# Softmax sums copied earlier, the first half's high part sooner and weight steps behind other tiles, in a fused attention and feed-forward kernel

## The chip, the cores and the metric

One core of a Trainium2 chip runs the whole program. Its engines run side by side, each through its own list of instructions in order: TensorE (matmuls, PE in the profile, its weight loads PEld), VectorE (DVE), ScalarE (ACT), GpSimd (POOL) and SyncE (SP), which issues most DMAs. The metric is the device time of one execution in microseconds, the median of several; lower is better.

## The reference

Attention over 16 heads of 576 positions and 64 dimensions with rotary embedding, then two feed-forward layers without gates over 1152 tokens (512 to 2048 to 512), the first with ELU, the second with Mish:

```python
q_rot, k_rot = (rotate(q), rotate(k))
scores = scale * np.matmul(q_rot, k_rot.transpose(0, 1, 3, 2))
scores = scores - np.max(scores, axis=-1, keepdims=True)
attn = np.exp(scores)
attn = attn / (np.sum(attn, axis=-1, keepdims=True) + 1e-09)
attn_out = np.matmul(attn, v)
...
x = attn_out.transpose(0, 2, 1, 3).reshape(B * S, H * D)
h = x @ w_in;  g = elu(h);           x = g @ w_out     # first layer
h = x @ w_in2; g = h * tanh(softplus(h)); out = g @ w_out2  # second layer
```

The weights come as 64-bit floats.

## The kernel before

All matmul operands of the feed-forward layers, and q and k, are held as a high part and a low part, and each product is made of three matmuls (high by high, high by low, low by high).

The attention takes the 16 heads in 8 pairs. A pair has 9 tiles of 128 queries (TPP = 9): tiles 0 to 3 are its first half (256 queries of both heads), tiles 4 to 8 its second half (320 queries of both heads; tile 8 holds the last 64 queries of either head). Tile number u counts through all pairs, u = 9 p + i. The engines' orders are written by hand: inside `manual_schedule` each engine executes what the Python loop emits, in that order. One turn of the loop (L573) at u does:

- TensorE: scores of tile u (`do_S`, into `ps_s`, two buffers). In pairs 0 and 1 an even tile issues the scores of two tiles at once, interleaved.
- VectorE: the maximum over the keys of tile u (`do_max`, writes `mn`, L392), and at tiles 4 and 0 the inverse of a finished half's sums (`do_inverse`, writes `rw`).
- TensorE: the transposes of tile u - 3 (LAG = 3): 512 keys into `psT` (L441, two buffers by turns), the last 64 keys into one of four slots of the single `psL` (L442).
- At tile 6, and at tile 2 of the next pair, the spread (`do_spread`, L423): matmuls that lay the inverse sums of a half out over `psA`. They need `psA` free, that is the product R before (L488) done.
- One turn later TensorE begins the weighted sums of that half (`do_av`, L473, two chunks of keys, and three more two turns later), into the same `psA`. Before that ScalarE must have copied the spread sums out of `psA` to R (`do_keep`, L432).
- ScalarE or VectorE copies `psT` to `pt` (`do_evac`, L455 on VectorE for tiles 0, 2, 4 and 8, in the last two pairs 0 and 4; else L457 on ScalarE). Behind tiles 3, 7 and 8 VectorE copies `psL` to `pt` (`do_evac_last`, L467), which frees its slots.
- ScalarE: exp of tile u (`do_exp`, L400), which gives P and its sums.
- After the last chunk of a half VectorE multiplies `psA` by R (`do_x`, L488); ScalarE rounds that to XH (`do_xh`, L492), and GpSimd makes XL, the low part (`do_xl`, L496).

GpSimd also does the rope products for the pair after next (L273 to L277) and the split of q and k of the next pair into high and low (L298, L299), whose results SP's DMAs stack.

In between stand weight steps: a job turns 512 KB of 64-bit weights (`raw`) into high and low parts. It is a product on GpSimd (L95, writes `wu`), three integer operations on VectorE (L99, L103, L107), and at last a rounding copy on ScalarE and a difference on GpSimd (L121, L122). `weight_part` does one such step, and keeps two jobs open, so that the GpSimd product of a job comes as soon as the job before it is opened or done. `PARTS` (L551 to L553) says how many steps stand at the end of which tile. 32 steps, 8 jobs, stand in the attention; the other jobs run in the feed-forward layers.

Of the kernel before, what the change touches and what calls it, by code (L numbers as in the profile page):

```python
# [21 lines left out]
def plain(ap):  # L22
    return ap.bitcast(F32)
# [3 lines left out]
def kernel(  # L27
# [11 lines left out]
    nc = tc.nc  # L39
    NP = qk.shape[0]  # L40
# [12 lines left out]
    TPP = 9  # L53
    NU = NP * TPP
# [76 lines left out]
    def prefetch_weights(n):  # L131
        while loaded[0] < min(len(jobs), opened[0] + n):
            load_weight(jobs[loaded[0]])
            loaded[0] += 1
# [95 lines left out]
    def attention(att, ps, tail):  # L230
# [32 lines left out]
        def load_v(p):  # L263
            v = att.tile([128, 5, 128], F32, tag="v", name="v_t", bufs=2)
            nc.sync.dma_start(out=v, in_=vp[p])
            v_t[p] = v
# [162 lines left out]
        def do_keep(p, g):  # L429
            n = (256, 320)[g]  # L430
            R_t[p, g] = att.tile([128, n], F32, tag=f"R{g}", name=f"R{g}", bufs=1)
            nc.scalar.activation(out=R_t[p, g], in_=psA[:, :n], func=AF.Copy)  # L432
# [11 lines left out]
        def do_evac(u):  # L444
            p, i = divmod(u, TPP)
            tv = psT[u % 2]
            pt = pt_t[0 if i < 4 else 1]
            if tiles[i] is not None:
                h, t = tiles[i]
                o = pt[:, h, 0:4, 128 * (t % 2):128 * (t % 2) + 128]  # L450
            else:
                o = pt[:, :, 0:4, 256:320].rearrange("p h c q -> p c h q")
                tv = tv.rearrange("p c (h q) -> p c h q", h=2)
            if i in (ON_DVE if p < NP - 2 else ON_DVE[::2]):
                nc.vector.tensor_copy(out=o, in_=tv)  # L455
            else:
                nc.scalar.activation(out=o, in_=tv, func=AF.Copy)  # L457

        def do_evac_last(i):
            r = S - 512  # L460
            if i < 8:
                o = pt_t[i // 4][:r, :, 4, 0:256].rearrange("p h (t q) -> p h t q", t=2)
                tv = psL[:r].rearrange("p (t h) q -> p h t q", h=2)
            else:
                o = pt_t[1][:r, :, 4, 256:320]
                tv = psL[:r, 0, :].rearrange("p (h q) -> p h q", h=2)
            nc.vector.tensor_copy(out=o, in_=tv)  # L467
# [12 lines left out]
        def x_parts(p, g):  # L480
            b, hp = divmod(p, HPB)
            q0 = (0, 256)[g]
            q1 = (256, S)[g]
            return R_t[p, g], XH[:, b, hp, q0:q1], XL[:, b, hp, q0:q1]
# [5 lines left out]
        def do_xh(p, g):  # L490
            x, hi, lo = x_parts(p, g)
            nc.scalar.activation(out=hi, in_=x, func=AF.Copy)  # L492

        def do_xl(p, g, eng):
            x, hi, lo = x_parts(p, g)
            eng.tensor_tensor(out=lo, in0=x, in1=plain(hi), op=ALU.subtract)  # L496
# [24 lines left out]
        def keep_warm(n):  # L521
            for _ in range(n):
                nc.tensor.matmul(psA[:, 0:128], lhsT=zero, rhs=zero, start=True, stop=True)
# [13 lines left out]
        def prepare(p, k):  # L537
            if k == 0:
                if p + 1 < NP:
                    load_pair(p + 1)  # L540
                split_alloc(p)
                split_half(p, 2, "kh", "kl")
                stack_k(p)
            elif k == 1:
                split_half(p, 0, "qh", "ql")
                stack_q(p)
            elif p + 1 < NP:
                rope_part(p + 1, 2 if k < 5 else 0, (k - 2) % 3, nc.gpsimd)

        LAG = 3  # L550
        PARTS = {u: 1 for u in (28, 30, 32, 34, 37, 39, 41, 43, 46, 48, 50, 52)}  # L551
        PARTS.update({u: 2 if u % 3 == 2 else 1 for u in range(54, 63)})
        PARTS.update({u: 1 for u in range(63, 71)})  # L553
        plan = {
            6: [("r", 0)], 7: [(0, 0), (0, 1)], 9: [(0, 2), (0, 3), (0, 4)],
            11: [("r", 1)], 12: [(1, 0), (1, 1)], 14: [(1, 2), (1, 3), (1, 4)],
# [9 lines left out]
        ends, spreads = {}, {}  # L566
# [6 lines left out]
        for u in range(max(av_at) + 2):  # L573
            p, i = divmod(u, TPP)
            for k in range(8):
                if p and i == k and p + 1 < NP:
                    prepare(p + 1, k)
            if u == 2:
                load_pair(2)
                split_alloc(1)  # L580
            if i == 8 and p + 1 < NP:
                load_v(p + 1)
            if u == 24:
                prefetch_weights(2)
            if u < NU:
                do_S(u)
            if u < LAG + 4:
                keep_warm(FILL[u])
            for (pp, g) in ends.get(u - 1, []):
                do_x(pp, g)  # L590
            if u < NU:
                do_max(u)
            if u == 1:
                first_lo(*HEAD[3])
            if 0 <= u - LAG < NU:
                do_T(u - LAG)
            if i == 4 and u < NU:
                do_inverse(p, 0)
            if i == 0 and u:
                do_inverse(p - 1, 1)  # L600
            for (pp, g) in spreads.get(u - 1, []):
                if u <= NU:
                    do_keep(pp, g)
            for (pp, g, c) in av_at.get(u, []):
                if g == "r":
                    do_spread(pp, c)
                else:
                    do_av(pp, g, c)
            if u >= NU:
                tail(u - NU, False)  # L610
            if 0 <= u - LAG < NU:
                do_evac(u - LAG)
                if (u - LAG) % TPP in (3, 7, 8):
                    do_evac_last((u - LAG) % TPP)
            for (pp, g) in spreads.get(u, []):
                if u >= NU:
                    do_keep(pp, g)
            if u < NU:
                do_exp(u)
            if u == 1:  # L620
                first_hi(*HEAD[-1])
                first_lo(*HEAD[-1])
                stack_q(0)
                nc.scalar.activation(out=tab[:, 0:2, :], in_=tab[:, 2:4, :], func=AF.Copy, scale=QSCALE)
                rope_half(1, 0, nc.gpsimd)
            if u in (3, 5):
                second_split(2 if u == 3 else 0)
            if u == 5:
                stack_q(1)
            if u in (6, 7, 8):  # L630
                for k in (2 * u - 10, 2 * u - 9):
                    prepare(1, k)
            for (pp, g) in ends.get(u - (1 if u >= NU else 2), []):
                do_xh(pp, g)
                do_xl(pp, g, nc.gpsimd if pp < NP - 1 else nc.vector)
            for _ in range(PARTS.get(u, 0)):
                if njob[0] < 2 * GF:
                    weight_part()
            if u >= NU:
                tmp_pool[0] = att  # L640
                tail(u - NU, True)
                tmp_pool[0] = None
# [225 lines left out]
```

## Time and profile before

| | us |
|---|---|
| median of 3 runs | 578.35 |
| the runs | 578.35, 583.51, 577.58 |
| profiled execution | 578.34 |
| its span, first to last instruction | 576.6 |
| TensorE matmul busy | 554.1 (96%) |
| VectorE, ScalarE, GpSimd busy | 374.1, 276.5, 240.9 |
| granted TensorE clock | 0.999 |

The busy time of an engine is a share of the whole span; a stage's limit has to be looked for in that stage. The attention takes about the first 163 us, the two layers the rest. Starts in the rows are microseconds from the first instruction. The end of a matmul in these rows is modelled, so the distance from one start to the next says more than the printed length.

### The profile page before, as it was taken

What the parts mean: (1) busy time and instruction counts of PE and PEld (TensorE: products, weight loads), DVE (VectorE), ACT (ScalarE), POOL (GpSimd) and SP (SyncE); (2) the same over time, 40 slices, a digit from 0 to 9 for tenths busy, and PEclk for the clock granted to TensorE, in tenths of its full rate; (3) what the DMA queues carried; (4) which work ended last, traced back from release to release, by engine and by line L of the source; (5) the groups of instructions that cost most, each with busy time, mean ns of one, the idle gap of its engine ahead of it and who ended that gap; (6) DMA issues with size and microseconds to landing.
All of it is one profiled execution on the core that took longest, in us unless ns stands there. A gap on an engine that the chain in (4) does not pass through costs nothing.

```text
span 576.6 us, 10135 instructions
## 1 busy us (share of the span) xinstructions
PE 554.1 (96%) x3888; PEld 499.3 (87%) x3888; DVE 374.1 (65%) x607; ACT 276.5 (48%) x512; POOL 240.9 (42%) x227
## 2 busy tenths in 40 slices
PE   7789999998999999999999999999999999999996
PEld 6567767776788999999999999999999998999985
DVE  5666778788845867677777777769934555442221
ACT  3646665666755755654554555534533322322110
POOL 6998889884310232233233232355543332230000
PEclk9999999999999999999999999999999999999999
DMA  6367766646210232222232222243542332100012
GB/s 227 112 190 213 228 202 160 197 121 181 73 38 1 74 110 74 79 106 73 75 111 74 74 81 103 59 138 119 164 124 84 107 99 97 33 14 10 28 64 92
DMA packets 43120, 60.69 MB, mean 105 GB/s; under 512 B 13760, under 2 KB 31936, under 8 KB 42304
## 3 DMA queue, kind: packets, MB, share of 16 engines
q1 hardware_dynamic: 42528, 59.46, 33.5%
q8 instruction: 31, 0.51, 0.4%
q10 hardware_dynamic: 544, 0.59, 0.3%
q14 instruction: 17, 0.14, 0.1%
HBM read 46.20 MB, written 2.36 MB: 84 GB/s over the span
## 4 chain that ended last, share of the span: by engine, by line
PE 86%; DVE 5%; ACT 5%; issue 2%; DMA 1%; POOL 0%; SPq 0%; ACTq 0%; POOLq 0%; DVEq 0%
PE ps_s L183 34%; PE ps_g L682 17%; PE ps_h L711 17%; PE psA L473 7%; PE ps_s L385 7%; PE psT L441 3%; DVE mn L392 2%; ACT P L400 2%; DMA qk_t<-in_qk_dram 1%; ACT R L432 1%; PE psL L442 1%; PE psA L423 1%; DVE pt L467 1%; ACT XH L492 0%; DVE tb L217 0%
## 5 line engine op out<-in xcount | busy, mean ns | idle before, releaser
L392 DVE TENSOR_REDUCE mn<-ps_s 128x1 f32<-128x576 f32 x72 | 54.0, 752 | 30.4 <-PE ps_s L385 30.2
L660 ACT ACTIVATE ta<-ps_s 128x576 f32<-128x576 f32 x32 | 20.8, 649 | 92.7 <-PE ps_s L183 92.7
L400 ACT ACTIVATE P<-ps_s,mn 128x576 f32<-128x576 f32 x72 | 53.2, 738 | 16.0 <-DVE mn L392 15.9
L183 PE MATMUL ps_s<-XH,wi0h 128*128 128x288 f32 x256 | 54.9, 296 | 0.9 <-DVE tb L218 0.9
L183 PE MATMUL ps_s<-XL,wi0h 128*128 128x288 f32 x256 | 54.5, 294 | 0.0
L183 PE MATMUL ps_s<-XL,wi1h 128*128 128x288 f32 x256 | 54.4, 294 | 0.0
L183 PE MATMUL ps_s<-XH,wi0l 128*128 128x288 f32 x256 | 54.4, 294 | 0.0
L183 PE MATMUL ps_s<-XH,wi1l 128*128 128x288 f32 x256 | 54.2, 293 | 0.0
L183 PE MATMUL ps_s<-XH,wi1h 128*128 128x288 f32 x256 | 54.2, 293 | 0.0
L122 POOL TENSOR_TENSOR wi1l<-wu,wi1h 128x512 fp32r<-128x512 f32 x16 | 21.4, 1338 | 78.2 <-ACT wi1h L121 78.2
L99 DVE TENSOR_SCALAR wu<-wu 128x512 int32<-128x512 int32 x64 | 32.8, 513 | 30.4 <-POOL wu L95 30.2
L473 PE MATMUL psA<-pt,v_t 128*64 128x256 f32 (+1 forms) x320 | 45.6, 416 | 6.1 <-ACT R L432 5.8
L107 DVE SCALAR_TENSOR_TENSOR wu<-raw,wu 128x512 int32<-128x512 int32 x64 | 49.0, 765 | 1.7
L122 POOL TENSOR_TENSOR wo0l<-wu,wo0h 128x512 fp32r<-128x512 f32 x16 | 21.8, 1365 | 61.9 <-ACT wo0h L121 50.3
L457 ACT ACTIVATE pt<-psT 128x512 f32<-128x512 f32 x44 | 26.3, 597 | 43.6 <-PE psT L441 43.6
L95 POOL TENSOR_SCALAR wu<-raw 128x512 f32<-128x512 f32 x64 | 45.0, 704 | 5.0
L103 DVE SCALAR_TENSOR_TENSOR wu<-raw,wu 128x512 int32<-128x512 int32 x64 | 45.9, 717 | 1.8
L122 POOL TENSOR_TENSOR wo1l<-wu,wo1h 128x512 fp32r<-128x512 f32 x16 | 22.0, 1375 | 57.3 <-ACT wo1h L121 57.0
L183 PEld LDWEIGHTS ps_s<-XH,wi0h 128*128 128x128 f32 x256 | 41.4, 188 | 3.2 <-DVE tb L218 1.3
L662 DVE TENSOR_TENSOR g<-ta,g 128x576 fp32r<-128x576 f32 x25 | 20.4, 817 | 36.5 <-ACT g L661 36.5
L441 PE MATMUL psT<-idn,P 128*128 128x128 f32 x288 | 43.4, 274 | 0.0
L183 PEld LDWEIGHTS ps_s<-XH,wi1h 128*128 128x128 f32 x256 | 41.7, 188 | 1.2
(146 smaller groups left out, 1408.6 us busy)
## 6 DMA issues: line engine op xcount, KB each, us to landing
raw<-in_w_in_dram SPq DMA_DIRECT2D x32, 512.0 KB, 3.7
raw<-in_w_out_dram SPq DMA_DIRECT2D x32, 512.0 KB, 3.3
qk_t<-in_qk_dram SPq DMA_DIRECT2D x6, 1152.0 KB, 5.4
qa<-qh SPq DMA_DIRECT2D x24, 144.0 KB, 2.7
v_t<-in_vp_dram SPq DMA_DIRECT2D x8, 320.0 KB, 3.1
out_dram<-Y SPq DMA_DIRECT2D x9, 256.0 KB, 2.0
ka<-kh SPq DMA_DIRECT2D x12, 144.0 KB, 2.4
ka<-kl SPq DMA_DIRECT2D x12, 144.0 KB, 2.8
```

The lines of the kernel that those rows point to most:

```text
L95: nc.gpsimd.tensor_scalar(out=u, in0=high.bitcast(F32), scalar1=REBASE, scalar2=0.0, op0=ALU.mult, op1=ALU.add)
L103: nc.vector.scalar_tensor_tensor(out=ui, in0=high, scalar=-0x80000000, in1=ui, op0=ALU.bitwise_and, op1=ALU.bitwise_or)
L107: nc.vector.scalar_tensor_tensor(out=ui, in0=low, scalar=29, in1=ui, op0=ALU.logical_shift_right, op1=ALU.bitwise_or)
L122: nc.gpsimd.tensor_tensor(out=lo, in0=u, in1=plain(hi), op=ALU.subtract)
L183: nc.tensor.matmul(o[:, j, :HS], lhsT=w[:, cc, :], rhs=x[:, b, cc, j * HS:j * HS + HS], start=(k == 0), stop=(k == 3 * NC - 1),)
L385: nc.tensor.matmul(psS[w][:, j, :HS], lhsT=l, rhs=r(slice(j * HS, j * HS + HS)), start=(a == 0), stop=(a == len(passes) - 1),)
L392: nc.vector.tensor_reduce(out=m, in_=psS[u][:, :, :HS], axis=AX.XY, op=ALU.min)
L400: nc.scalar.activation(out=P.rearrange("p (j n) -> p j n", j=2), in_=psS.pop(u)[:, :, :HS], func=AF.Exp, scale=-1.0, bias=mn_t.pop(u), acc ...
L441: nc.tensor.transpose(tv[:, c, :], P[:, c * 128:c * 128 + 128], idn)
L473: nc.tensor.matmul(o[64 * h:64 * h + 64, :n], lhsT=v_t[p][:, c, 64 * h:64 * h + 64], rhs=pt_t[g][:, h, c, :], start=(c == 0), stop=(c == 4),)
L682: nc.tensor.matmul(o[:, j, :HS], lhsT=w[:, e * 128:e * 128 + 128], rhs=gt[:, i, j * HS:j * HS + HS], start=(k == 0), stop=(k == 3 * GF - 1),)
L711: nc.tensor.matmul(o, lhsT=l, rhs=w, start=(k == 0), stop=(k == 3 * GF - 1))
```

## The change

Five edits in the loop over tiles:

1. The copy of the spread sums (`do_keep`) is emitted in the same turn as the spread, ahead of that tile's exp; before, it came one turn later, behind that exp.
2. XH and XL of a first half are emitted one turn after its last chunk, not two. The second half's stay.
3. Behind tile 8 VectorE copies `psL` ahead of `psT`.
4. The weight steps stand in every pair from pair 2 on: one at tiles 3 and 5 and two at tile 7 in pairs 2 to 5; two each at tiles 3, 5, 7 and 8 in pairs 6 and 7. Before, they stood at tiles 1, 3, 5 and 7 of pairs 3 to 5, at all tiles of pair 6 and at tiles 0 to 7 of pair 7. There are 32 steps as before.
5. The first two weight loads are issued at u = 16 (tile 7 of pair 1), not at u = 24.

```diff
-        PARTS = {u: 1 for u in (28, 30, 32, 34, 37, 39, 41, 43, 46, 48, 50, 52)}
-        PARTS.update({u: 2 if u % 3 == 2 else 1 for u in range(54, 63)})
-        PARTS.update({u: 1 for u in range(63, 71)})
+        PARTS = {}
+        for p in range(2, NP):
+            for i, n in ((3, 1), (5, 1), (7, 2)) if p < NP - 2 else ((3, 2), (5, 2), (7, 2), (8, 2)):
+                PARTS[TPP * p + i] = n
...
-            if u == 24:
+            if u == 16:
                 prefetch_weights(2)
...
-            for (pp, g) in spreads.get(u - 1, []):
-                if u <= NU:
-                    do_keep(pp, g)
...
             if 0 <= u - LAG < NU:
+                j = (u - LAG) % TPP
+                if j == 8:
+                    do_evac_last(j)
                 do_evac(u - LAG)
-                if (u - LAG) % TPP in (3, 7, 8):
-                    do_evac_last((u - LAG) % TPP)
+                if j in (3, 7):
+                    do_evac_last(j)
             for (pp, g) in spreads.get(u, []):
-                if u >= NU:
-                    do_keep(pp, g)
+                do_keep(pp, g)
             if u < NU:
                 do_exp(u)
...
-            for (pp, g) in ends.get(u - (1 if u >= NU else 2), []):
-                do_xh(pp, g)
-                do_xl(pp, g, nc.gpsimd if pp < NP - 1 else nc.vector)
+            for (pp, g) in ends.get(u - 1, []) + ends.get(u - 2, []):
+                if (pp, g) in ends.get(u - (2 if g and u < NU else 1), []):
+                    do_xh(pp, g)
+                    do_xl(pp, g, nc.gpsimd if pp < NP - 1 else nc.vector)
```

First place, ScalarE at the start of pair 4 (the numbers behind the names count tiles; R1_ is pair 3's second half, R0_ its first half; P is an exp). Before:

```order
L457 ACTIVATE pt1_86<-psT1_82 128x4x128
L400 ACTIVATE P_1120,sums2_78<-ps_s_1105,mn_1111 128x576
L400 ACTIVATE P_1145,sums2_78<-ps_s_1128,mn_1133 128x576
L492 ACTIVATE XH_61<-R0_1018 128x256
L432 ACTIVATE R1_1162<-psA_84 128x320
L400 ACTIVATE P_1169,sums2_78<-ps_s_1150,mn_1155 128x576
```

After:

```order
L457 ACTIVATE pt1_86<-psT1_82 128x4x128
L400 ACTIVATE P_1131,sums2_78<-ps_s_1116,mn_1122 128x576
L492 ACTIVATE XH_61<-R0_1013 128x256
L432 ACTIVATE R1_1153<-psA_84 128x320
L400 ACTIVATE P_1155,sums2_78<-ps_s_1136,mn_1141 128x576
```

XH and the copy of R stand ahead of the exp of tile 2, no longer behind it.

Second place, VectorE at the same seam (mn is a maximum, psT with 128x4x2x64 is tile 8). Before:

```order
L467 COPY pt1_86<-psL_83 64x2x256
L99 TENSOR_SCALAR wu_894<-wu_894 128x512
L392 TENSOR_REDUCE mn_1133<-ps_s_1128 128x1
L455 COPY pt1_86<-psT1_82 128x4x2x64
L467 COPY pt1_86<-psL_83 64x2x64
L392 TENSOR_REDUCE mn_1155<-ps_s_1150 128x1
L455 COPY pt0_85<-psT0_81 128x4x128
L103 SCALAR_TENSOR_TENSOR wu_894<-raw_756,wu_894 128x512
```

After:

```order
L467 COPY pt1_86<-psL_83 64x2x256
L392 TENSOR_REDUCE mn_1141<-ps_s_1136 128x1
L467 COPY pt1_86<-psL_83 64x2x64
L455 COPY pt1_86<-psT1_82 128x4x2x64
L392 TENSOR_REDUCE mn_1163<-ps_s_1158 128x1
L455 COPY pt0_85<-psT0_81 128x4x128
L99 TENSOR_SCALAR wu_949<-wu_949 128x512
```

The weight step at tile 1 is gone, the two copies behind tile 8 have changed places, and the first weight step stands where the second stood.

Third place, GpSimd in pair 2, behind the split of pair 3's q and k. Before:

```order
L299 TENSOR_TENSOR ql_601<-qk_t_362,qh_604 128x576
L273 TENSOR_TENSOR qk_t_597<-qk_t_597,tab_75 128x576
L496 TENSOR_TENSOR XL_62<-R0_567,XH_61 128x256
L275 TENSOR_TENSOR qk_t_597<-qk_t_597,tab_75 128x576
L277 TENSOR_TENSOR qk_t_597<-qk_t_597 128x576
```

After:

```order
L299 TENSOR_TENSOR ql_605<-qk_t_362,qh_608 128x576
L496 TENSOR_TENSOR XL_62<-R0_557,XH_61 128x256
L273 TENSOR_TENSOR qk_t_601<-qk_t_601,tab_75 128x576
L275 TENSOR_TENSOR qk_t_601<-qk_t_601,tab_75 128x576
L95 TENSOR_SCALAR wu_715<-raw_562 128x512
L95 TENSOR_SCALAR wu_719<-raw_564 128x512
L277 TENSOR_TENSOR qk_t_601<-qk_t_601 128x576
```

XL has moved ahead of the first rope product, and the products of the first two weight jobs stand among the rope products of this pair.

## Rows read from the trace of the kernel before

**Rows 1.** Waits of TensorE, from 160 us to the end: total, times, longest.

```profile
PE ps_s L183 <- DVE tb L218: 0.9, 2, 0.7
```

**Rows 2.** Waits in 18 to 164 us, the attention: total, times, longest.

```profile
DVE mn L392 <- PE ps_s L385: 29.7, 36, 2.0
...
PE psA L473 <- ACT R L432: 5.0, 9, 1.3
PE ps_s L385 <- ACT P L400: 3.5, 4, 1.1
PE psL L442 <- DVE pt L467: 2.1, 5, 0.5
```

**Rows 3.** Time line of TensorE, first scores of pairs 2, 3, 6, 7: start, length.

```profile
48.66 0.51 PE L385 MATMUL ps_s<-ka,qa 128*128 128x288 f32 x2
...
66.47 0.51 PE L385 MATMUL ps_s<-ka,qa 128*128 128x288 f32 x2
...
122.84 0.51 PE L385 MATMUL ps_s<-ka,qa 128*128 128x288 f32 x2
...
142.51 0.51 PE L385 MATMUL ps_s<-ka,qa 128*128 128x288 f32 x2
```

**Rows 4.** Time line of TensorE at the seam from pair 3 to pair 4.

```profile
90.35 0.78 PE L423 MATMUL psA<-idn,rw 128*128 128x128 f32 x6
...
91.54 0.60 PE L441 MATMUL psT<-idn,P 128*128 128x128 f32 x4
92.65 0.30 PE L442 MATMUL psL<-idn,P 128*64 128x128 f32 x1 [0.51 <-DVE pt L467]
93.42 1.30 PE L473 MATMUL psA<-pt,v_t 128*64 128x320 f32 x8 [0.46 <-ACT R L432]
94.65 0.53 PE L385 MATMUL ps_s<-ka,qa 128*128 128x288 f32 x2
...
96.36 0.60 PE L441 MATMUL psT<-idn,P 128*128 128x128 f32 x4
96.79 0.27 PE L442 MATMUL psL<-idn,P 128*64 128x128 f32 x1
97.00 1.84 PE L473 MATMUL psA<-pt,v_t 128*64 128x320 f32 x12
```

**Rows 5.** Time line of ScalarE at the same seam.

```profile
91.90 0.74 ACT L400 ACTIVATE P<-ps_s,mn 128x576 f32<-128x576 f32 x1 [1.34 <-DVE mn L392]
...
92.94 0.43 ACT L432 ACTIVATE R<-psA 128x320 f32<-128x320 f32 x1
```

**Rows 6.** Time line of TensorE, second half of pair 0.

```profile
37.49 1.30 PE L473 MATMUL psA<-pt,v_t 128*64 128x320 f32 x8 [0.36 <-ACT R L432]
```

**Rows 7.** Time line of VectorE, the seam to pair 4 and one quiet step.

```profile
90.08 1.06 DVE L99 TENSOR_SCALAR wu<-wu 128x512 int32<-128x512 int32 x1
...
91.73 0.68 DVE L455 COPY pt<-psT 128x512 f32<-128x512 f32 x1
92.33 0.27 DVE L467 COPY pt<-psL 64x128 f32<-64x128 f32 x1
...
98.15 1.01 DVE L107 SCALAR_TENSOR_TENSOR wu<-raw,wu 128x512 int32<-128x512 int32 x1
...
154.09 0.42 DVE L99 TENSOR_SCALAR wu<-wu 128x512 int32<-128x512 int32 x1
```

**Rows 8.** Time line of GpSimd in pair 2.

```profile
52.72 1.42 POOL L273 TENSOR_TENSOR qk_t<-qk_t,tab 128x576 f32<-128x576 f32 x1
55.52 0.73 POOL L496 TENSOR_TENSOR XL<-R,XH 128x256 fp32r<-128x256 f32 x1 [1.38 <-ACT XH L492]
```

**Rows 9.** The page: a group (busy, mean ns) and DMA issues (KB, us to landing).

```profile
L95 POOL TENSOR_SCALAR wu<-raw 128x512 f32<-128x512 f32 x64 | 45.0, 704 | 5.0
...
raw<-in_w_in_dram SPq DMA_DIRECT2D x32, 512.0 KB, 3.7
...
qk_t<-in_qk_dram SPq DMA_DIRECT2D x6, 1152.0 KB, 5.4
```

## The prediction

> **What bounds the kernel now.** TensorE does, nearly everywhere, so only moments in which TensorE stands still are worth anything. I first read the list of waits. After the attention, in the two feed-forward layers, TensorE waits 0.9 us for an engine with work that this change does not touch [rows 1]; a microsecond saved in the attention is therefore a microsecond at the end, and nothing later gives it back. In the stretch of the attention in which the change acts (18 to 164 us) two waits are aimed at: the weighted sums (psA, L473) wait for ScalarE's copy of the inverse sums (R, L432), 5.0 us in 9 places, and the transposes of the last 64 keys (psL, L442) wait for VectorE's copy of the previous psL (L467), 2.1 us in 5 places [rows 2]. VectorE itself waits 29.7 us for scores in the same stretch [rows 2], so it has room, but not in every tile.
>
> Then I read TensorE's time line, at the first score matmul of each pair. Pair 2, which has no weight steps on VectorE, takes 66.47 - 48.66 = 17.81 us; pairs 3 to 5 take (122.84 - 66.47) / 3 = 18.79 us each; pair 6, with the most weight steps, 19.67 us [rows 3]. The matmuls are the same, so 1.0 to 1.9 us per pair is waiting, and it goes with the weight steps.
>
> Third, the place itself, the start of pair 4 [rows 4]. Undisturbed, psL starts 0.43 us after the first of the four psT transposes (96.36 to 96.79) and the weighted sums 0.21 us after psL (97.00). At the seam from one pair to the next the same steps take 1.11 us (91.54 to 92.65) and 0.77 us (93.42). So 0.68 + 0.56 = 1.24 us are lost, where the list shows 0.51 and 0.46 us of idle time: each listed wait costs 0.1 to 0.17 us more than its idle time. Taking 1.24 us off 18.79 gives 17.55 us, close to what pair 2 takes now less its own small wait: the floor of a pair is about 17.5 us, and no pair can win more than brings it there.
>
> **The sums copied ahead of the exp.** Before, ScalarE had exp, XH, copy of R, exp in this row: exp at 91.90, the copy at 92.94, ready at 93.37; TensorE's weighted sums start at 93.42, directly behind it [rows 4, 5]. The copy needs the spread matmuls (L423), which end at 90.35 + 0.78 = 91.13 [rows 4]. Copied directly then, R is ready at 91.13 + 0.43 = 91.56, before TensorE could use it (91.97 + 0.21 = 92.18, if psL does not wait). The wait goes, in all 9 places: 5.0 us of idle time and 9 times 0.1 us, 5.9 us. The matching copies of the first halves in pairs 2 to 7 show no wait in this list, and I count nothing for them.
>
> What is queued behind the copy: the exp of the same tile now stands behind a wait for the spread. At this seam it starts at 91.56 instead of 91.90 (it had been late for VectorE's maximum, see below), lasts 0.74 us and ends at 92.30; the scores that need its buffer are those of tile 4, before at 94.65, after the gain of 1.24 us at 93.41 [rows 4, 5]. That leaves 1.1 us, so it costs nothing here. In pairs 0 and 1 there is no such room: two tiles' scores are issued together there and the later one waits for an exp, which is most of the 3.5 us of TensorE's wait for P (L400) [rows 2]. At the one second half there (the wait of 0.36 us before 37.49 [rows 6]) the exp of the tile after would end about where it ends now; I leave 0.4 us of the 5.9 where it is: 5.5 us.
>
> XH of the first half moves one tile forward, into ScalarE's idle time behind the exp of tile 1 (ScalarE waits 1.34 us before 91.90 [rows 5]): nothing on the path, but on GpSimd XL now stands ahead of all the rope products.
>
> **The psL copy ahead of the psT copy, and the weight steps elsewhere.** On VectorE the weight step at tile 1 takes 1.06 us from 90.08, then come the maximum, the psT copy at 91.73 and the psL copy, 92.33 to 92.60 [rows 7]; psL on TensorE starts at 92.65, right behind [rows 4]. Without the weight step this runs about 1.0 us earlier and, with the two copies exchanged, the psL copy 0.60 us earlier still (92.33 - 91.73): ready near 91.0, and TensorE wants it at 91.97. What is late next is the psT copy of tile 8, which must be ready for the weighted sums at 92.18: it now follows, takes 0.67 us and ends near 91.7, 0.5 us ahead. So all of the 2.1 us and 5 times 0.16 us go, 2.9 us; pairs 6 and 7 now have weight steps in tiles 7 and 8, which can push back the psL copy of tile 7 a little, and I leave 0.2 us: 2.7 us. Together 5.5 + 2.7 = 8.2 us.
>
> The steps are as many as before, 8 jobs with the same instructions; the new places, tiles 3, 5 and 7, lie beside the weighted sums, during which VectorE waits for the next scores. The first step of a job takes 0.42 us where GpSimd is quiet (154.09) and 1.06 us beside it [rows 7]. At tile 3 of pair 4 the transposes of tile 0 end at 91.54 + 0.60 = 92.14 [rows 4]; behind them come the end of a maximum and a copy of 0.6 to 0.7 us, so VectorE is free at about 93.0, and the scores of tile 4 end at about 93.41 + 0.8 = 94.2: either length fits.
>
> **The cost: pair 2.** Weight steps begin a pair sooner, in the one pair that was clean, and there the first step on VectorE waits for GpSimd's first product of the same job (L95), which was issued in the same tile. GpSimd's queue before it: XL, which waits for XH, then two rope products. In the trace of before GpSimd starts a rope product at 52.72 directly after the split, and XL at 55.52 after waiting 1.38 us [rows 8]. XH comes one tile sooner, which is at least one exp (0.74 us [rows 5]) and at most the 1.38 us that GpSimd waited; with 1.2 us XL starts near 54.3, and then 0.73 + 2 x 1.42 + 0.70 = 4.3 us pass to the end of the first product [rows 8, 9]: about 58.6 by the old clock. VectorE gets there 7.7 us behind the start of the pair, as worked out above for pair 4 (93.0, and pair 4 starts at 66.47 + 18.79 = 85.26 [rows 3]), that is near 56.4. It stands still for about 2 us, with tile 4's maximum queued behind it, for whose exp the scores of tile 6 wait, and later the product R (L488), for which the next spread waits. Of that its idle time covers about half (29.7 us in 36 waits, 0.8 us each [rows 2]). The bounds are nothing (GpSimd in time) and 4.3 us (all of its row waited for); I take 1.0 us, since the idle wait lies directly behind.
>
> The two weight loads now issued ahead of the loads of v and q/k in pair 1 cost SP's queue a few instructions; they matter only by the last rival.
>
> **The sum.** The profiled execution is 578.34 us, 1.74 us over its span, and the median of the three runs is 578.35, so no correction is needed: 578.3 - 8.2 + 1.0 = **571.1 us**.
>
> **Rivals.** (a) *The cost of pair 2 does not come, and the first halves give a little:* if GpSimd is there in time, and the unlisted waits for first-half copies add half a microsecond, 578.3 - 8.2 - 0.5 = 569.6. For it: VectorE's idle time; against: GpSimd is the fullest queue of pairs 2 to 5.
>
> (b) *VectorE is held by GpSimd in the new places.* The trace shows that the two hold each other up: the same step takes 0.42 or 1.06 us, and the third step at 98.15 takes 1.01 us [rows 7] beside rope products of 1.42 us [rows 8]. If each of pairs 3 to 5 has one step held for a whole rope product, 1.42 us less the 0.3 us that the third step already suffers, 1.1 us lands on VectorE's row to the product R and the spread: 3 x 1.1 = 3.3 us, 574.4 us. Against it: the phase between the two engines is set anew in each pair by XL, and the old places had such meetings too. The Trainium skill (SBUF — State Buffer, section "Who interferes with whom") states that VectorE with two SBUF inputs, or in a two-port mode, and GpSimd share a port pair which the first to issue keeps for its whole instruction, while the other blocks. The two lengths of the first step agree with that; by it alone every step that meets a rope product would be held, and the sum would be this rival's.
>
> (c) *Slower.* The chain of pair 2 at its full length: the two weight loads stand on SP ahead of the q/k load that GpSimd's rope products of pair 2 read; they land 3.7 us after their issue each, the q/k load 5.4 us [rows 9]. If they delay it by 2 x 3.7 = 7.4 us in full, the two rope products wait, the weight product behind them too, and VectorE stands for 7.4 + 4.3 = 11.7 us, of which 0.8 us is covered: 578.3 - 8.2 + 10.9 = 581.0. It decides against the change from 9 us of standing on. Against it: before, the same two weight loads stood ahead of the next pair's q/k load, and the list of waits of that stretch has no GpSimd wait for a load.
>
> **Chances.** The forecast 0.60 (570.2 to 572.5), (a) 0.15, (b) 0.19, (c) 0.06. A measurement of this kernel can tell about 1%, 5.8 us, so faster means under 572.6: forecast and (a), 0.75; within 1% is (b), 0.19; slower (c), 0.06. The range reaches over (a) and (b), 569.2 to 574.5.
>
> **What would show it.** In the profile after: the psA wait for R in 18 to 157 us nearly gone (under 1 us) and the psL wait under 0.5 us; pairs 3 to 6 at 17.5 to 17.8 us each, pair 2 longer than before, with a wait of VectorE's L99 for GpSimd's L95 of about 2 us. The step on pair 2 is wrong if that wait is under 0.5 us or over 4. I would be wrong on the whole if TensorE waits for exp (ps_s <- P) in pairs 2 to 7, where it has 1.1 us of room, or if pairs 3 to 5 stay above 18.3 us because VectorE's row has become the bound.

## The result, and the profile after

The changed kernel takes 573.48 us, the median of 4 runs (570.46, 576.09, 570.94, 576.01), against 580.31 of the kernel before on the same chip (577.58 to 583.51): a ratio of 0.986, 95% interval 0.981 to 0.990, so 1.4% faster. Runs of most kernels here lie on two levels 4 to 6 us apart, a difference that the profiles show in the first feed-forward layer; so edits are compared below by the attention's stretches in the profiles, which repeat within 0.05 us where the instructions around them and the granted clock are the same, and not by medians.

The profiled execution took 570.46 us, its span 568.6 us (before: 578.34 and 576.6). The list of waits of the changed kernel from 17 to 158 us (total, times, longest):

```profile
DVE mn L392 <- PE ps_s L385: 14.7, 23, 2.0
...
PE ps_s L385 <- ACT P L400: 4.5, 6, 1.1
...
DVE wu L99 <- POOL wu L95: 2.6, 1, 2.6
...
PE psA L423 <- DVE R L488: 0.7, 1, 0.7
```

Both waits of [rows 2] that the change aimed at are gone: TensorE waits neither for R nor for psL. Two rows are new: VectorE's weight step waits once for GpSimd, and a spread waits for the product R. VectorE's wait for scores has halved, from 29.7 us.

TensorE's time line, first scores of pairs 2, 3, 6 and 7 and the first matmul of the feed-forward layers (start, length):

```profile
46.81 0.38 PE L385 MATMUL ps_s<-ka,qa 128*128 128x288 f32 x1
...
65.95 0.38 PE L385 MATMUL ps_s<-ka,qa 128*128 128x288 f32 x1
...
119.42 0.38 PE L385 MATMUL ps_s<-ka,qa 128*128 128x288 f32 x1
...
136.87 0.38 PE L385 MATMUL ps_s<-ka,qa 128*128 128x288 f32 x1
...
156.57 0.53 PE L183 MATMUL ps_s<-XH,wi0h 128*128 128x288 f32 x2
```

Against [rows 3] pair 2 is longer (65.95 - 46.81 = 19.14 us, before 17.81), pairs 3 to 5 take 17.82 each (18.79), pair 6 17.45 (19.67). In all kernels run here no pair from pair 2 on takes less than 17.44 us; that is the floor which the prediction put near 17.5.

The seam to pair 4, TensorE, and the next spread:

```profile
90.05 0.60 PE L441 MATMUL psT<-idn,P 128*128 128x128 f32 x4
90.49 0.27 PE L442 MATMUL psL<-idn,P 128*64 128x128 f32 x1
90.69 1.30 PE L473 MATMUL psA<-pt,v_t 128*64 128x320 f32 x8
...
97.11 0.27 PE L442 MATMUL psL<-idn,P 128*64 128x128 f32 x1
97.49 0.49 PE L423 MATMUL psA<-idn,rw 128*128 128x128 f32 x2
```

psL comes 0.44 us after psT and the weighted sums 0.20 us after psL, the undisturbed distances of [rows 4]; all 1.24 us lost there are back. The spread comes 0.38 us after psL (0.11 us in e5_tile6 below), and this is what is late now. VectorE at the same place:

```profile
89.25 0.27 DVE L467 COPY pt<-psL 64x128 f32<-64x128 f32 x1
89.45 0.67 DVE L455 COPY pt<-psT 128x512 f32<-128x512 f32 x1
...
91.53 1.70 DVE L99 TENSOR_SCALAR wu<-wu 128x512 int32<-128x512 int32 x1
...
95.81 1.23 DVE L103 SCALAR_TENSOR_TENSOR wu<-raw,wu 128x512 int32<-128x512 int32 x1
96.96 0.48 DVE L488 TENSOR_TENSOR R<-psA,R 128x320 f32<-128x320 f32 x1
```

The first step takes 1.70 us, longer than either length of [rows 7], and the second 1.23 us; directly behind the second stands the product R, for which the spread waits. GpSimd starts rope products at 91.53 and 95.08:

```profile
91.53 1.41 POOL L275 TENSOR_TENSOR qk_t<-qk_t,tab 128x576 f32<-128x576 f32 x1
92.92 0.82 POOL L95 TENSOR_SCALAR wu<-raw 128x512 f32<-128x512 f32 x1
...
95.08 1.41 POOL L273 TENSOR_TENSOR qk_t<-qk_t,tab 128x576 f32<-128x576 f32 x1
96.45 1.86 POOL L275 TENSOR_TENSOR qk_t<-qk_t,tab 128x576 f32<-128x576 f32 x1
```

Pair 2, GpSimd, then VectorE, then TensorE:

```profile
52.49 0.73 POOL L496 TENSOR_TENSOR XL<-R,XH 128x256 fp32r<-128x256 f32 x1 [0.99 <-ACT XH L492]
53.82 1.41 POOL L273 TENSOR_TENSOR qk_t<-qk_t,tab 128x576 f32<-128x576 f32 x1 [0.59 <-DMA qk_t<-in_qk_dram]
...
56.57 1.31 POOL L95 TENSOR_SCALAR wu<-raw 128x512 f32<-128x512 f32 x2
```

```profile
57.28 0.87 DVE L99 TENSOR_SCALAR wu<-wu 128x512 int32<-128x512 int32 x1 [2.63 <-POOL wu L95]
```

```profile
59.79 0.53 PE L385 MATMUL ps_s<-ka,qa 128*128 128x288 f32 x2 [0.64 <-ACT P L400]
...
61.86 0.71 PE L423 MATMUL psA<-idn,rw 128*128 128x128 f32 x4 [0.73 <-DVE R L488]
```

This is the forecast chain: XL and two rope products, then the weight products, VectorE still for 2.63 us, and then both scores and spread late. One link is additional: GpSimd waits 0.59 us for the q/k load, issued at 45.41 behind the two weight loads and landed at 53.75.

### The profile page after: what moved, and what is told of

The parts are those of the page before. It is cut to its first block, busy times and chain, and to the rows that moved or that the text cites. A ratio compares the mean times of both kernels' runs of the same rounds, so it can differ in the third digit from the quotient of the medians.

```text
span 568.6 us, 10131 instructions
## 1 busy us (share of the span) xinstructions
PE 553.9 (97%) x3888; PEld 499.7 (88%) x3888; DVE 376.9 (66%) x607; ACT 277.9 (49%) x512; POOL 238.7 (42%) x227
## 4 chain that ended last, share of the span: by engine, by line
PE 85%; DVE 6%; ACT 3%; DMA 2%; issue 1%; POOL 1%; SPq 1%; ACTq 0%; POOLq 0%; DVEq 0%
PE ps_s L183 34%; PE ps_g L683 18%; PE ps_h L712 17%; PE ps_s L385 5%; PE psA L473 5%; PE psT L441 4%; DMA qk_t<-in_qk_dram 2%; PE psA L423 2%; DVE mn L392 1%; ACT P L400 1%; DVE wu L99 1%; PE psL L442 1%; DVE pt L455 1%; DVE R L488 0%; DVE rw L411 0%
## 5 line engine op out<-in xcount | busy, mean ns | idle before, releaser
L99 DVE TENSOR_SCALAR wu<-wu 128x512 int32<-128x512 int32 x64 | 33.7, 527 | 32.9 <-POOL wu L95 32.9
L107 DVE SCALAR_TENSOR_TENSOR wu<-raw,wu 128x512 int32<-128x512 int32 x64 | 48.8, 762 | 1.7
L103 DVE SCALAR_TENSOR_TENSOR wu<-raw,wu 128x512 int32<-128x512 int32 x64 | 47.6, 744 | 2.0
L95 POOL TENSOR_SCALAR wu<-raw 128x512 f32<-128x512 f32 x64 | 45.1, 706 | 4.7
```

Of the source, the lines that this page charges most:

```text
L95: nc.gpsimd.tensor_scalar(out=u, in0=high.bitcast(F32), scalar1=REBASE, scalar2=0.0, op0=ALU.mult, op1=ALU.add)
L99: nc.vector.tensor_scalar(out=ui, in0=ui, scalar1=3, scalar2=0x7FFFFFF8, op0=ALU.logical_shift_left, op1=ALU.bitwise_and)
L103: nc.vector.scalar_tensor_tensor(out=ui, in0=high, scalar=-0x80000000, in1=ui, op0=ALU.bitwise_and, op1=ALU.bitwise_or)
L107: nc.vector.scalar_tensor_tensor(out=ui, in0=low, scalar=29, in1=ui, op0=ALU.logical_shift_right, op1=ALU.bitwise_or)
```

## The experiments

Lengths of the pairs in us, from one pair's first scores to the next's (pair 7: to the first feed-forward matmul). Pair 0 is left out here, because in some of these profiles the granted clock fell within it (e2_steps: 0.71 from 21 to 24 us, e1_copies: 0.50 from 12 to 15 us; before and changed: 1.00 throughout).

| kernel | 1 | 2 | 3 | 4 | 5 | 6 | 7 | sum |
|---|---|---|---|---|---|---|---|---|
| before | 21.19 | 17.81 | 18.79 | 18.79 | 18.80 | 19.67 | 20.92 | 135.97 |
| changed | 20.29 | 19.14 | 17.82 | 17.82 | 17.83 | 17.45 | 19.71 | 130.06 |
| e1_copies | 20.58 | 17.44 | 18.56 | 19.05 | 19.05 | 18.29 | 19.95 | 132.92 |
| e2_steps | 21.20 | 18.81 | 17.81 | 17.83 | 17.81 | 17.82 | 20.00 | 131.28 |
| e3_psl | 21.21 | 17.80 | 18.83 | 18.79 | 18.80 | 19.67 | 20.93 | 136.03 |
| e4_products | 20.29 | 17.45 | 17.44 | 18.16 | 17.84 | 17.45 | 19.70 | 128.33 |
| e5_tile6 | 20.29 | 17.45 | 17.45 | 17.45 | 17.45 | 17.45 | 19.71 | 127.25 |
| e6_xh_late | 20.58 | 19.79 | 17.45 | 17.45 | 17.45 | 17.45 | 19.71 | 129.88 |
| e7_psl_last | 20.27 | 18.52 | 17.83 | 17.84 | 17.83 | 17.45 | 19.69 | 129.43 |
| e8_tile6_late | 20.90 | 17.56 | 17.57 | 17.56 | 17.57 | 17.55 | 20.00 | 128.71 |
| e9_seam | 21.19 | 17.81 | 18.45 | 17.81 | 17.81 | 19.67 | 20.93 | 133.67 |
| e10_load | 20.27 | 18.54 | 17.83 | 17.83 | 17.83 | 17.46 | 19.71 | 129.47 |

The prediction's account, that each listed wait is a gain of its own, is theory A in e1_copies, e2_steps, e8_tile6_late and e9_seam, and the rival in e3_psl. Each ratio is to the kernel before on the same chip.

**e1_copies**: the kernel before with edit 1 alone.

```diff
-            for (pp, g) in spreads.get(u - 1, []):
-                if u <= NU:
-                    do_keep(pp, g)
...
             for (pp, g) in spreads.get(u, []):
-                if u >= NU:
-                    do_keep(pp, g)
+                do_keep(pp, g)
```

> The kernel before with edit 1 alone: the copy of the spread sums stands ahead of the exp of the same tile, everything else as before. Theory A (each place where TensorE stands still costs its listed idle time and 0.1 to 0.17 us, and the copy of R is late by its place in ScalarE's order): the psA wait for R goes in the whole attention but for the one behind its last tile, the psL wait stays; a profiled span about 5.8 us shorter than the 576.6 us before, 570.8, and pairs 3 to 5 at 18.2 us. Theory B (the copy was late only because the weight steps on VectorE made the maximum and so the exp ahead of it late): only the places without weight steps gain, pairs 0 to 2, some 1.5 us; a span of 575.

Measured: median 578.12, ratio 0.992 (0.989 to 0.996). The wait for R is gone everywhere, but pairs 4 and 5 are longer than before, 19.05 us. TensorE and VectorE there:

```profile
110.79 0.30 PE L442 MATMUL psL<-idn,P 128*64 128x128 f32 x1 [0.83 <-DVE pt L467]
111.02 1.30 PE L473 MATMUL psA<-pt,v_t 128*64 128x320 f32 x8
```

```profile
107.89 1.39 DVE L99 TENSOR_SCALAR wu<-wu 128x512 int32<-128x512 int32 x1
```

The sums follow psL at once, so the copy is in time; but the weight step of tile 1, 1.06 us in [rows 7], meets GpSimd otherwise and takes 1.39, and the wait for psL grows from 0.51 to 0.83. So in pairs 3 to 5, three of the nine places of theory A, the copies win nothing. They win in pairs 1 (0.61), 2 (0.37), 6 (1.38) and 7 (0.97), together 3.05 us, about half of what theory A expected. Theory B falls too: it gave the gain to pairs 0 to 2 alone, and pairs 6 and 7, full of weight steps, win most.

**e2_steps**: the kernel before with edits 4 and 5 alone.

```diff
-        PARTS = {u: 1 for u in (28, 30, 32, 34, 37, 39, 41, 43, 46, 48, 50, 52)}
-        PARTS.update({u: 2 if u % 3 == 2 else 1 for u in range(54, 63)})
-        PARTS.update({u: 1 for u in range(63, 71)})
+        PARTS = {}
+        for p in range(2, NP):
+            for i, n in ((3, 1), (5, 1), (7, 2)) if p < NP - 2 else ((3, 2), (5, 2), (7, 2), (8, 2)):
+                PARTS[TPP * p + i] = n
...
-            if u == 24:
+            if u == 16:
```

> The kernel before with edits 4 and 5 alone: the weight steps in their new tiles and the first two weight loads sooner. Theory A: the psL waits go with the steps (about 2.8 us), the R waits shrink to those of pair 2, 0.18 us each, but the ones in pairs 0 and 1 stay (together 2.6 us), and pair 2 (about 1.6 us) and the third step's meetings with GpSimd (0.8 us) are paid: a span about 3 us shorter, 573.6. Theory B: all of the gain is here, a span near 568.6.

Measured: median 576.98, ratio 0.989 (0.983 to 0.995). Pairs 3 to 5 are as in the changed kernel, with the copies behind the exp. The listed waits for R fall from 5.0 to 1.9 us though no copy was moved. The 4.69 us that pairs 1 to 7 win lie between theory A (3) and theory B (8): neither holds.

**e3_psl**: the kernel before with edit 3 alone.

```diff
             if 0 <= u - LAG < NU:
+                j = (u - LAG) % TPP
+                if j == 8:
+                    do_evac_last(j)
                 do_evac(u - LAG)
-                if (u - LAG) % TPP in (3, 7, 8):
-                    do_evac_last((u - LAG) % TPP)
+                if j in (3, 7):
+                    do_evac_last(j)
```

> The kernel before with edit 3 alone: behind tile 8 the psL copy ahead of the psT copy. Theory A: at the seams the psL wait shrinks by up to 0.5 us, but the copy of R ends when it ended before and the weighted sums start behind it all the same, so their wait grows by as much: span 576.6 within 0.3 us. Rival: each wait counts by itself, and four seams give 0.65 us each: 574.0.

Measured: median 582.23, ratio 0.999 (0.996 to 1.003). The wait for psL falls to 0.6 us, the wait for R rises to 6.2; no pair changes by more than 0.04 us, so the rival, the prediction's own way of counting, falls. The two waits of a seam stand one behind the other.

**e4_products**: the changed kernel, and GpSimd's products of the first two jobs opened two tiles sooner.

```diff
+            if u == 2 * TPP + 1:
+                open_job()
+                open_job()
             for _ in range(PARTS.get(u, 0)):
```

> The changed kernel with GpSimd's products of the first two weight jobs two tiles sooner, at tile 1 of pair 2, ahead of that pair's rope products; VectorE's steps stay where they are. Theory A (pair 2 pays 1.3 to 1.6 us because VectorE's first step waits 2.6 us for GpSimd's product): that wait goes, pair 2 takes 17.6 to 17.9 us and not 19.15, span 567.1. Rival (pair 2 pays because the DMA engines are full there, share 0.96, and q and k come late): pair 2 stays at 19.1 us, span 568.6.

Measured: median 573.13, ratio 0.985 (0.979 to 0.990). VectorE's wait for L95 is gone, pair 2 takes 17.45: the chain read off the rows costs 19.14 - 17.45 = 1.69 us, all of it this wait. So the rival with the full DMA engines falls. But pair 4 is longer by 0.34, so the sum falls by 1.73 only and the medians do not tell the two kernels apart. VectorE in pair 2, then in pair 4, and TensorE there:

```profile
54.43 1.62 DVE L99 TENSOR_SCALAR wu<-wu 128x512 int32<-128x512 int32 x1
...
58.63 0.74 DVE L103 SCALAR_TENSOR_TENSOR wu<-raw,wu 128x512 int32<-128x512 int32 x1
...
89.32 0.65 DVE L99 TENSOR_SCALAR wu<-wu 128x512 int32<-128x512 int32 x1
...
93.21 1.96 DVE L103 SCALAR_TENSOR_TENSOR wu<-raw,wu 128x512 int32<-128x512 int32 x1
```

```profile
95.62 0.71 PE L423 MATMUL psA<-idn,rw 128*128 128x128 f32 x4 [0.45 <-DVE R L488]
```

In both pairs L103 stands directly ahead of the product R. Pair 2, where the first step is held and this one is not, is at the floor; pair 4, where the first is short and this one takes 1.96 us, is 0.71 us over it.

**e5_tile6**: e4_products with the second weight step of pairs 2 to 5 at tile 6.

```diff
-            for i, n in ((3, 1), (5, 1), (7, 2)) if p < NP - 2 else ((3, 2), (5, 2), (7, 2), (8, 2)):
+            for i, n in ((3, 1), (6, 1), (7, 2)) if p < NP - 2 else ((3, 2), (5, 2), (7, 2), (8, 2)):
```

> The changed kernel with two further edits: the first two weight products on GpSimd are opened at tile 1 of pair 2, so that VectorE finds them done (the edit of e4_products), and the second weight step of pairs 2 to 5 stands at tile 6 instead of tile 5. Theory C (formed after the first four runs: in pairs 3 to 6 it is VectorE's row, with its steps held by GpSimd, that sets the length of a pair, and the late product R holds the next spread): pairs 2 to 5 all near 17.45 us, no wait of the spread for the product R over 0.2 us; pairs 1 to 7 sum to 127.5 (128.3 with the products alone, 130.1 in the changed kernel), profiled execution about 567 to 568 in its quicker level, ratio to before about 0.981. Rival D (the meeting with GpSimd only moves to another step): at least one of pairs 2 to 5 stays at 17.8 or above, the sum at 128.2 to 129, no difference from e4_products.

Measured: median 570.0 (567.56 to 572.44), ratio 0.978 (0.974 to 0.982): the best kernel here. Its interval just touches the changed kernel's, but the attention is shorter by 130.06 - 127.25 = 2.8 us. Pairs 2 to 6 all take 17.45. VectorE and TensorE in pair 4:

```profile
89.95 1.69 DVE L99 TENSOR_SCALAR wu<-wu 128x512 int32<-128x512 int32 x1
...
94.65 0.49 DVE L488 TENSOR_TENSOR R<-psA,R 128x320 f32<-128x320 f32 x1 [0.35 <-PE psA L473]
```

```profile
95.54 0.27 PE L442 MATMUL psL<-idn,P 128*64 128x128 f32 x1
95.65 0.61 PE L423 MATMUL psA<-idn,rw 128*128 128x128 f32 x4
```

The first step is held as long as before, 1.69 us, and costs nothing, although a maximum stands directly behind it: VectorE even waits for the sums ahead of the product R, and the spread follows psL after 0.11 us. With the two pairs of e4_products this shows that a held first step alone costs nothing, and that the 0.37 us per pair came with the hold of the second step, directly ahead of R.

**e8_tile6_late**: e5_tile6 with the copies of the sums behind the exp again (edit 1 undone).

> e5_tile6 without the copies of the sums moved: they stand behind the exp again as in the kernel before. Tells whether the copy ahead of the exp is worth anything once VectorE's row has been shortened. Theory A (each second half's copy behind the exp holds the weighted sums by 0.5 to 0.7 us): pairs 2 to 5 at 17.45 + 0.4 to 0.6, that is 17.85 to 18.05, the sum of pairs 1 to 7 3.0 to 4.0 us above e5_tile6, waits of psA for R of 0.4 to 0.6 us in 7 places. Rival E (VectorE's row is all that matters, the copies then come in time because the exp before them is earlier too): under 0.1 us per pair in 2 to 5, and only pairs 0 and 1 longer, the sum at most 1.0 us above e5_tile6.

Measured: median 575.3, ratio 0.987 (0.986 to 0.989). Pairs 2 to 6 are longer by 0.10 to 0.12, pair 1 by 0.61, pair 7 by 0.29, the sum by 1.46. Theory A with 3 to 4 us falls; rival E is near, a little too low. The list of waits, 17 to 158 us, and ScalarE and TensorE at the seam:

```profile
PEld psA L473 <- ACT R L432: 4.8, 15, 0.7
...
PE psA L473 <- ACT R L432: 0.7, 2, 0.5
```

```profile
89.84 0.74 ACT L400 ACTIVATE P<-ps_s,mn 128x576 f32<-128x576 f32 x1
...
90.57 0.43 ACT L432 ACTIVATE R<-psA 128x320 f32<-128x320 f32 x1
```

```profile
90.91 0.27 PE L442 MATMUL psL<-idn,P 128*64 128x128 f32 x1
91.11 1.30 PE L473 MATMUL psA<-pt,v_t 128*64 128x320 f32 x8
```

The copy starts at 90.57, ends at 91.00, and the sums start 0.20 us after psL, undisturbed: behind the exp, and in time, because the exp ahead no longer waits (1.34 us in [rows 5]) and XH no longer stands between them (edit 2): the copy starts 0.73 us after the exp, and 1.04 us after it in e9_seam, where XH is still there. Note the row of 4.8 us: it is the weight loader's, beside matmuls that still run, and it costs at most the 0.10 to 0.12 us per pair.

**e6_xh_late**: the changed kernel without edit 2.

```diff
-            for (pp, g) in ends.get(u - 1, []) + ends.get(u - 2, []):
-                if (pp, g) in ends.get(u - (2 if g and u < NU else 1), []):
-                    do_xh(pp, g)
-                    do_xl(pp, g, nc.gpsimd if pp < NP - 1 else nc.vector)
+            for (pp, g) in ends.get(u - (1 if u >= NU else 2), []):
+                do_xh(pp, g)
+                do_xl(pp, g, nc.gpsimd if pp < NP - 1 else nc.vector)
```

> The changed kernel without the step that makes the first half's XH one tile sooner. Prediction's step: on the path it costs nothing by itself, its effect is that XL stands ahead of the rope products on GpSimd. Theory A: pairs 3 to 5 within 0.1 us of 17.82; in pair 2 GpSimd starts with the rope products at the landing of the q/k load (53.75 in the changed kernel's profile), XL behind them, so the first weight product ends at 53.75 + 2.8 + 0.73 + 0.7 = 58.0 against 57.9: pair 2 within 0.2 us of 19.1 to 20.3 (the changed kernel's). Rival B (XL's place decides which VectorE step meets GpSimd): at least one of pairs 3 to 6 differs by 0.3 us or more from the changed kernel, up or down.

Measured: median 574.68, ratio 0.984 (0.980 to 0.988). Rival B: XL's place shifts GpSimd's row, and pairs 3 to 5 fall to 17.45. VectorE's two steps in pair 4 (the changed kernel: 1.70 and 1.23 us):

```profile
92.13 0.77 DVE L99 TENSOR_SCALAR wu<-wu 128x512 int32<-128x512 int32 x1
...
96.03 0.70 DVE L103 SCALAR_TENSOR_TENSOR wu<-raw,wu 128x512 int32<-128x512 int32 x1
```

Pair 2 is longer by 0.65 and pair 1 by 0.29; together edit 2 costs 130.06 - 129.88 = 0.18 us.

**e7_psl_last**: the changed kernel without edit 3.

> The changed kernel with the copy of psL behind the copy of psT of tile 8 again, as before the change. Prediction's step: the exchange makes psL ready 0.60 us sooner, on top of 1.0 us from the weight step that is gone from the seam. Theory A: with the weight step gone the copy is in time in either order (it had 0.9 us of room), so pairs 2 to 6 are within 0.1 us of the changed kernel's and the wait of psL for pt stays under 0.5 us in sum. Rival F (the seam is still tight on VectorE): waits of psL for pt of 0.3 us or more in 4 or more places, pairs 3 to 6 longer by 0.3 us each, 1.5 us in sum.

Measured: median 573.32, ratio 0.984 (0.979 to 0.989). Pairs 3 to 7 are the changed kernel's within 0.02 us. Pair 2 is shorter by 0.62, and not by the edit: pair 0 was longer in this profile (18.77 us), the q/k load had landed before GpSimd came, and the wait of 0.59 us is missing.

**e9_seam**: the kernel before, with the weight steps of pairs 3 to 5 at tiles 3, 5 and 7 (two).

```diff
-        PARTS = {u: 1 for u in (28, 30, 32, 34, 37, 39, 41, 43, 46, 48, 50, 52)}
+        PARTS = {TPP * p + i: n for p in (3, 4, 5) for i, n in ((3, 1), (5, 1), (7, 2))}
```

> The kernel before, with one thing changed: in pairs 3 to 5 the weight steps stand behind tiles 3, 5 and 7 instead of tiles 1, 3, 5 and 7; the copies of the sums stay behind the exp, pairs 2, 6 and 7 are as before. Theory G (the copy of R was late at the seam only because the exp ahead of it waited for a maximum that stood behind the weight step of tile 1, so that one microsecond is shown as a wait for R and can be had by either edit, but not twice): pairs 3 to 5 fall from 18.8 to 17.6 to 17.85 with the copies left where they were, the waits of the weighted sums for R fall from 5.0 us to under 2.5 us, pairs 2, 6 and 7 within 0.15 us of 17.81, 19.67 and 20.92, the sum of pairs 1 to 7 near 132.9. Theory A (the place of the copy itself costs 0.56 to 0.65 us per seam): pairs 3 to 5 at 18.2 to 18.4, the waits for R still 4 us or more, the sum near 134.3.

Measured: median 579.92, ratio 0.995 (0.993 to 0.998). Pairs 4 and 5 fall to 17.81, by 0.98 us each, with all copies where they were; pair 3, the first with steps, to 18.45, because its first step waits 1.8 us for GpSimd. So the cost of pair 2 goes to pair 3 here, with the first steps. Theory A is wrong by 0.4 to 0.6 us in pairs 4 and 5 and theory G right there, but G missed pair 3 and the waits for R, which are still 4.1 us. What is left at the seam of pair 4 is small, ScalarE and TensorE:

```profile
90.19 0.74 ACT L400 ACTIVATE P<-ps_s,mn 128x576 f32<-128x576 f32 x1 [0.35 <-DVE mn L392]
...
91.23 0.43 ACT L432 ACTIVATE R<-psA 128x320 f32<-128x320 f32 x1
```

```profile
91.26 0.27 PE L442 MATMUL psL<-idn,P 128*64 128x128 f32 x1
91.71 1.30 PE L473 MATMUL psA<-pt,v_t 128*64 128x320 f32 x8 [0.18 <-ACT R L432]
```

The exp ahead of the copy waits 0.35 us for its maximum and not 1.34, and the sums start 0.45 us after psL and not 0.77. The 0.25 us still lost are XH, which ScalarE does between that exp and the copy, as the comparison with e8_tile6_late shows.

**e10_load**: the changed kernel with the two weight loads issued behind the q/k load.

```diff
                     load_pair(p + 1)
+                if p == 3:
+                    prefetch_weights(2)
                 split_alloc(p)
...
-            if u == 16:
-                prefetch_weights(2)
```

> The changed kernel with the q/k load of the pair after next issued ahead of the first two weight loads on SyncE's queue instead of behind them. Prediction's rival of the weight loads (they delay the q/k load, the rope products behind it and so the first weight step): the load lands under 7 us after its issue instead of 8.34, GpSimd's wait of 0.6 us for it is gone, VectorE's first weight step waits for GpSimd's product about 2.0 us instead of 2.6, and pair 2 takes 18.5 us instead of 19.14; the weight loads land in time for the products. Rival (the load is late because of all the traffic then, not because of its place): the wait stays within 0.2 us of 0.6, pair 2 within 0.15 us of 19.14.

Measured: median 575.17, ratio 0.989 (0.985 to 0.993). Pair 2 takes 18.54, as expected, and the q/k load lands 5.4 us after its issue, not 8.3. GpSimd:

```profile
52.97 0.74 POOL L496 TENSOR_TENSOR XL<-R,XH 128x256 fp32r<-128x256 f32 x1 [0.93 <-ACT XH L492]
53.67 1.42 POOL L273 TENSOR_TENSOR qk_t<-qk_t,tab 128x576 f32<-128x576 f32 x1
```

The rope product starts right behind XL, VectorE's wait falls to 2.0 us. Of the 1.69 us of pair 2, 0.60 are the load and 1.09 GpSimd's row.

## Why the prediction was right, and where not

**The total.** Forecast 571.1 us; the profiled execution, to which the sum was made, took 570.46, the median 573.48, inside the range. From the first scores to the feed-forward layers the change won (163.43 - 9.71) - (156.57 - 9.33) = 6.5 us, forecast 7.2. The other 1.5 us of the span's 8.0 lie outside: 0.4 ahead of the first scores, where nothing was changed, and 1.1 behind the attention. Of the latter edit 1 gives some 0.3: at the slower rate of the first layer (last section) five kernels with it need 416.32 to 416.40 us from there to the end, three without it 416.61 to 416.71. The rest is not explained; e3_psl, whose code there is that of before, was 0.8 us shorter as well. That the total came so close is in good part luck. Without pair 2's cost and the holds of pairs 3 to 5 the same stretch wins 9.3 us (e5_tile6: 135.97 - 127.25 in pairs 1 to 7 and 0.57 in pair 0) and not 8.2; pair 2 cost 0.7 us more than forecast, the holds took 1.1 us that stood only in a rival, and the 1.5 us outside were in no term.

**The copies, 5.5 us: the step that failed.** "The wait goes in all 9 places" held, but the gain was put down to the wrong edit. At the seams of pairs 3 to 5 the copy was late because the exp ahead of it waited for a maximum, and that stood on VectorE behind the weight step of tile 1. Taking the step away gives 0.98 us per pair without any copy moved (e9_seam); moving the copies alone gives 0.23 us in pair 3 and loses 0.25 in pairs 4 and 5 (e1_copies). The prediction had the row, 1.34 us of waiting ahead of the exp [rows 5], and used it only for the length of the queue. On top of well placed steps and the earlier XH the copies are worth 1.46 us in pairs 1 to 7 (e8_tile6_late against e5_tile6): 0.61 in pair 1, where TensorE issues two tiles' scores together, 0.29 in the last, and 0.56 in the five pairs between. Pair 0, 17.76 before (17.79 in e9_seam) and 17.19 after, adds 0.57.

**psL and the weight steps, 2.7 us: too low by the same error.** Edits 4 and 5 alone win 135.97 - 131.28 = 4.69 us, although pair 2 loses 1.00 by them. The exchange of the two copies, the other half of this term, is worth nothing, with the old places of the steps (e3_psl: the copy of R ends the wait) and with the new ones (e7_psl_last: psL is in time either way). The copies alone, 3.05, and the steps alone, 4.69, overlap: all five edits give 5.91. Most of the overlap is in pairs 6 and 7, where they win 3.23 and 1.89 one by one and 2.22 and 1.21 together.

**XH sooner, counted at nothing.** That it moves XL ahead of the rope products was right, but this has a price: 0.37 us in each of pairs 3 to 5, by the step that it lets GpSimd hold (e6_xh_late). Pair 1 wins 0.29 us and pair 2 0.65. Where the copy of R stands behind the exp, XH is on the path (e9_seam).

**Pair 2, 1.0 us: right mechanism, 1.69 us.** VectorE's wait was 2.63 us, forecast 2; the 0.6 us too little are the q/k load, which the prediction had only in its rival of 581.0. That rival's link is real (e10_load), but the load came 0.59 us late for GpSimd and not 7.4.

**VectorE held by GpSimd, the rival of 574.4.** It happens, for 1.1 us in all and not 3.3: pairs 3 to 5 stay 0.37 us over the floor. The step that starts beside a rope product at 91.53 ends at 93.23, 0.3 us after that product gives way to the next instruction at 92.92. VectorE's copy ahead of the step ran until 90.93 + 0.68 = 91.61, so GpSimd was first. The Trainium skill (SBUF — State Buffer, section "Who interferes with whom") says that VectorE in a two-port mode contends with GpSimd, and that the first to issue keeps the shared port pair for its whole instruction; these rows agree. What the rival overrated is the price: two steps are held in each of these pairs, by 1.28 us over the quiet length of 0.42 and by 0.56 over 0.67, and 0.37 us of it reaches TensorE. A hold costs what VectorE's row cannot make up before TensorE needs its next result: nothing for the first step in pair 2 of e4_products and in e5_tile6, 0.71 us for the one directly ahead of R in pair 4 of e4_products.

**Signs to look for.** Both waits gone, pairs 3 to 6 between 17.45 and 17.83, the new wait of L99: as forecast. TensorE's wait for an exp in pair 2 (0.64 us) was named as a sign of being wrong on the whole, and it came. It does not come from the copy ahead of the exp, for which the sign was meant, but from VectorE's stop: in e4_products, without the stop, no TensorE wait for an exp is left behind pair 1.

## What to carry to other kernels

A wait in the list names who came last, not who was late: follow the releaser back over its own idle time, here from the copy over the exp and the maximum to a weight step on another engine, before giving the gain to the edit that moves the last link. Two edits that remove the same microsecond add up to less than their parts, so cost them one on top of the other. A filler step on an engine with idle time goes where that engine next waits for others, and not directly ahead of something that others wait for: here a step held to four times its length was free in the one place, and a shorter hold cost 0.37 us per pair in the other.

## What was not expected of the hardware

TensorE's rate in the first feed-forward layer has two values in these profiles at the same granted clock, 1.00. The window from 200 to 250 us of the changed kernel, then of e10_load (busy time and instructions of each engine, granted clock, DMA share, GB/s):

```profile
200.00:250.00 50.00, 50.00 (x387) 50.00 (x386) 35.01 (x51) 28.66 (x47) 15.97 (x16) 1.00 0.27 85
```

```profile
200.00:250.00 50.00, 50.00 (x377) 50.00 (x376) 34.75 (x51) 27.46 (x44) 15.94 (x16) 1.00 0.28 85
```

TensorE waits for nothing in either, and does 387 or 377 matmuls, 129 or 133 ns each, with the same code there. No kernel was profiled at both rates, so that the rate belongs to the execution and not to the kernel is not shown; what sets it stays open.

VectorE's L99 was found at 0.42, 0.77, 1.06, 1.39 and 1.70 us, among others, for the same 128x512 operation, by what GpSimd was at then: a step's length is not a constant of the step. All but the shortest end 0.28 to 0.29 us after the GpSimd instruction that they met: 91.14 after 90.86 before the change, 109.28 after 109.00 in e1_copies, 93.23 after 92.94 in the changed kernel, 91.64 after 91.36 in e5_tile6, 92.90 after 92.62 in e6_xh_late.
